# A new order table, and other buffer counts, for a fused gated-recurrence and spatial-gating kernel

## The chip, the cores and the metric

The kernel runs on one core of a Trainium2 chip. The metric is the device time of one execution in microseconds (us); the number given for a kernel is the median of its runs. A core has engines that run side by side, each through its own instruction stream in order: PE (TensorE, matrix products; its weight loads are listed as PEld), DVE (VectorE), ACT (ScalarE), POOL (GpSimd) and SP (SyncE, which here only issues transfers). Engines wait for each other through semaphores. Because a stream is executed in order, an instruction that waits holds back everything behind it on its engine.

## What is computed

The reference has two stages. The first is a gated linear recurrence over 768 steps for 4 batches of 8 heads of width 48; the second is a gated unit whose gate mixes the 768 positions with one 768 x 768 matrix. Cut to what matters:

```python
# stage 1, q, k, v, alpha: [4, 8, 768, 48]
for t in range(768):
    state = alpha[:, :, t, :, None] * state + k[:, :, t] (outer) v[:, :, t]
    y[:, :, t] = q[:, :, t] @ state
x = y.transpose(0, 2, 1, 3).reshape(4, 768, 384)
# stage 2, w_in [384, 1024], w_spatial [768, 768], w_out [512, 384]
h = maximum(x @ w_in, 0)
u, v = h[..., :512], h[..., 512:]
v_n = (v - mean(v)) / sqrt(var(v) + 1e-6)          # over the 512 features
v_s = einsum('ts,bsd->btd', w_spatial, v_n) + b_spatial[None, :, None]
out = (u * v_s) @ w_out
```

## The kernel before

Stage 1 is cut into chunks of 128 steps, six to a batch, 24 in all (numbered 0 to 23). The first eight chunks are loaded and worked on two at a time, as pairs 0 to 3 (function `pair`, line 414); the others singly (function `first`, line 625). For a chunk or a pair the steps are these.

- Four loads: `ac` (alpha), `kc`, `qc`, `vc` (lines 432 and 637, issued by SP). A pair's load is 384 KB, a single chunk's 192 KB. Each name has three buffers that hold two chunks.
- ACT takes the logarithm of alpha (`la`, L443). PE forms its running sums (`cump`, L452). ACT takes two exponentials of them, `binv` (L460) and one in place (L469). `kt` is k times the first (L474, POOL or DVE), `qt` is q times the second (L481, DVE).
- PE transposes `kt` and `qt` (L502), and DVE or ACT copies the results out as `kqT` (L198, L200). PE forms the scores (`sc`, L574), which DVE masks into `ptm` (`m`, L585). PE adds the chunk's contribution to the state (`updq`, L536 and L544). DVE adds the state before to it (`z`, L328, L330), POOL scales it (`S`, L335) and copies it for PE as `sbd` (`sb`, L200).
- PE forms the chunk's output from `ptm` and from the state (`ya`, L601, and `y`, L614). It is copied out (`xs`), transposed (`xt`, L365), and copied into `xT` (`xe`), which is x transposed, ready for stage 2.

For single chunks the same steps stand at L651 to L773, with DVE's `ptm` at L756, `kt` at L681 and `qt` at L691.

Stage 2 works per batch, all its products through one helper line (L819). `v` (24 products in three parts, `second_v`, line 858) makes a tile `v_sb` of 128 positions by 512 features. Its statistics are taken on DVE (`bn`, L884, L885; on ACT for four of them) and ACT (`rs`, L908), and DVE makes the normalised `vn` (L916) of it. `u` (32 products, `second_u`, line 933) makes `uT`. `s` (32 products, each in two halves of three parts, `second_s`, line 945) multiplies `vn` with the transposed spatial matrix `w_spT`. DVE adds the bias into `vsb` (L967), and POOL or DVE multiplies by `uT` into `gT` (`g`, L980). `o` (24 products, `second_o`, line 1017) multiplies with `w_out`. Its result is copied out and stored (L1037; the last tile in two halves, L1011). A matrix part with 512 columns moves 512/384 of the columns of the others.

Weights arrive in fp32 through two buffers called `raw_w` (`NRAW`, line 159) in six loads of 768 KB: `w_in` half 1 (for `v`), `w_in` half 0 (for `u`), `w_sp` 0, 1, 2 (two row blocks each of the spatial matrix), `w_out` (L1084). Each is cast to bf16 in pieces on POOL, ACT or DVE. A load into a buffer waits until the casts of the load before it in the same buffer are done. The spatial rows are transposed by PE (`wt`, L831) and copied out (`we`). `raw_w` buffers are later used for output tiles.

Nothing is scheduled when the kernel is built. Every step is an operation with a number, and the table `PLAN` (line 57) lists all 1156 in the order in which they are emitted: a letter for the engine (P, D, A, G for POOL, S for SP, Q for the landing of a transfer) and the number. The order on each engine is the order of its letters in the table. Numbers behind a colon add filler products to a PE operation: an fp32 product of a constant tile `junk`, of so many columns, that writes into the bank which the operation takes next (L188). Nothing reads its result; it is in PE's stream ahead of the operation. A filler shows as two matmuls in the trace.

Of the kernel before, what the change touches and what calls it, by code (L numbers as in the profile page):

```python
# [57 lines left out]
D0 S49 Q50 D7 D13 S109 Q110 G47 Q48 D11 S51 Q52 G9 D3 S55 Q56 D1 G8 D15 D17 G14 D6 D4 D2 D12 G16 S53 Q54 A57 S113 Q114  # L58
G18 A117 P118:512:512:192 S111 Q112 P68 A119 P262 A69 P58 S19 Q20 P264 G71 A59 P128 A120 A60 G61 S115 Q116 A70 D62
A129 D72 A265 D5 S178 Q179 A263 D122 A130 P126:512:512:512 D132 S180 Q181 G131 P76 P74 P64 P66 D75 G63 A65 D77 G73 D67  # L60
D127 G121 P89:504 P134 S182 Q183 D90 P136 P78 A135 D91 A137 P86 S184 Q185 G133 D80 A23 P124 D88 P149 A79 A125 G81 D87
A123 S322 Q323 G22 D83 A186 P92:512 D151 G82 P146 D93 G21 P96 P187 D150 A97 G84 P197 S24 Q25 A188 P94 D148 P138 G85
A95 D147 A189 G190 P98 S326 Q327 P100 A198 D191 A99 G200 A199 D140 P103 S324 Q325 A101 D201 G202 P195 A139 A192 D102
P203 G141 P193 A104 P205 P207 G142 D143 A194 D196 A206 P152 G144 D204 S29 Q30 D105 A330 S382 Q383 G145 P153 P157 P215
A154 D158 G10 P212 A208 A106 D209 P155 P341 D213 A156 G210 P159 P331 D214 A160 P161 A332 D216 G28 P172 A342 D217 G211
A333 A343 D335 G27 P218 A173 D345 G26 A162 P223 P219 D174 P349 A224 P339 S33 Q34 G334 P170 A220 S328 Q329 D350 P225
D163 P221 S384 Q385 P166 G344 A226 A222 P164 D167 A175 P337 P230 D171 A165 A338 D107 P227 D177 A231 D108 S386 Q387
P168 A390 D176 D340 A228 D32 P347 A169 P238 D31 A348 D229 P247 A239 P244 P362 S37 Q38 A245 P236 D248 A246 D249 G35
P240 D364 A237 S424 Q425 P242 A346 D363 G336 A241 P250 G36 D232 P391 A252 P351 A393 A243 D251 S426 Q427 P253 A233 D353
P270 A392 D234 P266 S428 Q429 A352 A255 D235 G354 P274 D254 A395 P275 D356 G355 D396 P271 G394 D276 P267 D272 S388  # L70
Q389 P359 D268 P398 P278 A39 G40 D360 S41 Q42 P279 D361 A399 G277 P256 A400 P259 D280 P365 G273 A432 D258 P405 S430
Q431 D257 A260 D261 P369 P433 A366 G357 P294 D370 S461 Q462 A434 G281 D406 P367 A435 P371 P295 S495 Q496 A372 D407
G397 P290 A437 G358 D296 P376 A368 D438 G269 P401 P408 P291 G436 A409 S499 Q500 P282 A377 D292 P410 A43 S465 Q466 P440
D402 D44 P283 A46 G403 D442 A412 P373 D441 A411 G45 D284 G439 P447 D378 S463 Q464 A469 P418 G297 A374 P470 D449 S467
Q468 P306 A503 G293 A471 D419 P504 P298 S497 Q498 A472 A307 D448 G285 A505 P420 D375 S592 Q593 A474 G404 P286 A507
D475 P443 A299 S598 Q599 G473 P287 D508 A421 P413 D444 S626 Q627 D288 G445 P416 A414 S501 Q502 G506 P450 A417 P422
D415 A451 S596 Q597 G476 P477 A379 P510 G289 P452 A423 D478 P302 S594 Q595 D453 A512 D479 G446 P480 D511 A600 S705
Q706 P484 D481 A454 P513 A303 D485 P601 G482 P314 A602 D486 G483 A634 P310 D514 S663 Q664 G509 A603 A315 P487 D515
G607 A605 P455 S667 Q668 A488 D606 A311 P516 D381 S665 Q666 A456 P489 D380 P318 A517 D604 S630 Q631 A490 D457 P518
A491 P608 A520 P611 S707 Q708 A519 P492 D319 A671 A458 D609 P521 S628 Q629 D610 A493 D459 P615 A522 D460 P528 D612  # L80
A494 D617 P672 G613 P532 A523 S709 Q710 D529 P635 A673 D616 P544 S777 Q778 A674 A713 G675 P530 D524 A676 P534 S632
Q633 A637 A636 D677 G614 P540 A525 S669 Q670 P714 A533 D526 P548 A639 D527 P560 S711 Q712 A531 D638 A716 P541 A715
D640 S873 Q874 P545 A718 G717 D542 A535 P549 S749 Q750 D546 P618 P561 D719 G547 A619 S743 Q744 D550 P642 A785 P679
D562 A641 P620 G543 P552 S779 Q780 A643 D644 P645 D622 P553 A621 G720 D680 S747 Q748 A681 D646 G678 P649 D554 P721
G647 S877 Q878 P686 D650 A722 P623 G551 D651 S781 Q782 P682 P556 A624 D683 P557 A723 D687 G684 P652 G555 D558 P536
S879 Q880 A653 D688 P537 A751 G648 S745 Q746 P654 P728 D538 G563 A656 P786 P724 D655 S783 Q784 P689 D730 A787 P564
G539 A690 D729 S907 Q908 P752 D725 P691 G685 A754 A789 P576 S946 Q947 A692 D790 A753 P565 D788 S875 Q876 P657 A756
G755 D693 A577 D566 P731 S944 Q945 A758 D757 P568 G559 A732 D625 S1023 Q1024 A658 P792 P759 G726 A569 P733 D794 P694
# [16 lines left out]
A1086 P1097 A1094 D1088 P1101 D1087 P1109 D1092 P1110 P1121 D1111 P1106 G1112 P1102 D1107 P1114 D1103 P1117 D1108  # L105
G1104 P1118 D1115 P1098 D1119 P1122 G1116 D1099 P1125 D1123 P869 D1100 G1124 P1126 D870 P1136 G1120 D1127 S871 Q872
P1128 D1137 P1148 A1129 S1138 Q1139 P1140 D1149 S1130 Q1131 P1132 A1141 S1150 Q1151 P1144 S1142 Q1143 A1133 P1152
S1134 Q1135 A1145 A1153 S1146 Q1147 S1154 Q1155
"""


# [1048 lines left out]
```

## Time and profile before

| | |
|---|---|
| median of 3 runs | 141.3 us (141.24 to 141.33) |
| span of the profiled execution | 144.3 us |
| PE busy | 136.8 us (95%) |
| DVE busy | 118.7 us (82%) |
| ACT busy | 106.8 us (74%) |
| POOL busy | 86.8 us (60%) |
| moved by DMA | 28.64 MB, mean 198 GB/s |

The profiled execution is 3.0 us longer than the median of the runs shown; its span is from its first instruction to its last, the stretch before the first load and the end of the program included. A timeline line gives start, duration, engine, source line, operation, tiles written and read, the number of instructions merged into it, and in brackets the idle time ahead of it with what ended it. A line of the windows view gives, for a stretch, the length, the busy time of PE, PEld, DVE, ACT and POOL with instruction counts, PE's granted clock, the DMA engines' mean busy share, and GB/s. A matmul's recorded duration runs on after the next one has begun, so a matmul's pace is read from starts, or from the length of a run of many.

### The profile page before, as it was taken

The numbers are of one execution on the slowest core, as the hardware profiler recorded it, in microseconds if no ns is written. First come the engines' busy times: TensorE is split into PE (matmuls) and PEld (weight loads), VectorE is DVE, ScalarE is ACT, GpSimd is POOL, SyncE is SP. The second block draws the span as 40 slices with busy tenths as digits, with TensorE's granted clock in tenths as the row PEclk, the third lists the DMA queues.
The fourth block names the chain that finished last, engine by engine and source line by source line (L and its number), as shares of the span: only waits on it lengthen the run. The fifth ranks groups of instructions, "written<-read, shape, count | busy, mean of one in ns | idle before, by whom it ended". The sixth has DMA issues, their size and how long they took to land.

```text
span 144.3 us, 4963 instructions
## 1 busy us (share of the span) xinstructions
PE 136.8 (95%) x1915; PEld 84.2 (58%) x1915; DVE 118.7 (82%) x289; ACT 106.8 (74%) x278; POOL 86.8 (60%) x152
## 2 busy tenths in 40 slices
PE   7799999799799999999999999999999999999990
PEld 3334766656465765676556665665657666555560
DVE  7015798899999969899999999999979897987940
ACT  3473479899895879899997789998797698861031
POOL 6856179892709979981249789511599687002820
PEclk9999999999999999999999999999999999999998
DMA  4999999929899989999899899799999241090055
GB/s 108 321 326 351 282 250 325 344 58 259 181 269 191 300 164 182 205 181 214 169 211 222 175 174 185 152 204 196 212 239 227 66 172 55 0 354 28 5 191 191
DMA packets 89000, 28.64 MB, mean 198 GB/s; under 512 B 83728, under 2 KB 87440, under 8 KB 88976
## 3 DMA queue, kind: packets, MB, share of 16 engines
q1 hardware_dynamic: 88944, 28.32, 79.5%
q8 instruction: 15, 0.25, 0.7%
q14 instruction: 9, 0.07, 0.1%
q0 software_dynamic: 32, 0.00, 0.0%
HBM read 23.60 MB, written 4.72 MB: 196 GB/s over the span
## 4 chain that ended last, share of the span: by engine, by line
PE 78%; DVE 8%; ACT 5%; DMA 3%; issue 3%; SPq 0%; ACTq 0%; DVEq 0%
PE bank L819 47%; PE bank L188 4%; DMA ac<-in_alpha_dram 3%; PE bank L710 3%; PE bank L452 2%; PE bank L502 2%; PE bank L745 2%; PE bank L574 2%; DVE ptm L756 2%; PE bank L773 2%; PE bank L731 2%; PE bank L544 1%; DVE ptm L585 1%; PE bank L657 1%; PE bank L601 1%
## 5 line engine op out<-in xcount | busy, mean ns | idle before, releaser
L819 PE MATMUL bank<-w_spT,vn 128*128 128x384 bf16 x192 | 36.3, 326 | 0.1
L980 POOL TENSOR_TENSOR gT<-vsb,uT 128x384 bf16<-128x384 f32 x28 | 25.7, 927 | 11.7 <-DVE vsb L967 11.2
L335 POOL TENSOR_TENSOR state<-state,bc 128x192 f32<-128x192 f32 x20 | 10.3, 513 | 21.4 <-DVE state L328 6.2
L819 PEld LDWEIGHTS <-vn 128*128 128x128 bf16 x192 | 17.1, 97 | 10.2 <-issue 0.2
L756 DVE TENSOR_TENSOR ptm<-bank,mask 128x512 bf16<-128x512 f32 x32 | 20.8, 682 | 1.0 <-ACT xT L198 1.0
L819 PE MATMUL bank<-xT,w_in 128*128 128x384 bf16 x96 | 19.4, 326 | 0.0
L967 DVE TENSOR_TENSOR vsb<-bank,bsp_bc 128x384 f32<-128x384 f32 x31 | 16.7, 554 | 3.2 <-PE bank L819 2.8
L819 PE MATMUL bank<-w_in,xT 128*128 128x512 bf16 x72 | 18.8, 379 | 0.0
L198 ACT COPY kqT<-bank 128x512 bf16<-128x512 bf16 x24 | 13.6, 590 | 6.9 <-PE bank L502 4.4
L819 PE MATMUL bank<-w_out_sb,gT 128*128 128x384 bf16 (+1 forms) x100 | 18.4, 320 | 0.1
L681 POOL TENSOR_TENSOR kt<-kc,binv 128x384 bf16<-128x384 f32 x13 | 12.0, 927 | 6.6 <-ACT bc L676 2.7
L200 POOL CAST sbd<-state 64x192 bf16<-64x192 f32 x40 | 13.6, 341 | 2.1
L884 DVE BATCH_NORM_STATS2 stats<-v_sb 128x6 f32<-128x512 bf16 x20 | 13.6, 681 | 0.5 <-ACT v_sb L204 0.5
L204 ACT ACTIVATE v_sb<-bank 128x512 bf16<-128x512 f32 x20 | 11.9, 608 | 1.6 <-PE bank L819 1.6
L198 ACT CAST x_sb<-bank 128x384 bf16<-128x384 f32 x21 | 10.2, 493 | 3.5 <-PE bank L773 2.7
L819 PEld LDWEIGHTS <-w_in 128*128 128x128 bf16 x96 | 8.7, 97 | 6.0
L188 PE MATMUL bank<-junk 128*128 128x512 f32 (+2 forms) x16 | 11.1, 838 | 1.1 <-DVE halves_of L264 1.1
L200 DVE COPY kqT<-bank 128x512 bf16<-128x512 bf16 x24 | 9.2, 415 | 3.1 <-PE bank L502 2.3
L819 PEld LDWEIGHTS <-gT 128*128 128x128 bf16 x100 | 8.7, 97 | 5.1 <-POOL gT L980 0.2
L204 ACT ACTIVATE uT<-bank 128x384 bf16<-128x384 f32 x23 | 11.3, 495 | 0.3 <-PE bank L819 0.2
L198 ACT COPY xT<-bank 128x192 bf16<-128x192 bf16 (+1 forms) x27 | 9.1, 378 | 2.4 <-PE bank L365 1.5
L585 DVE TENSOR_TENSOR ptm<-bank,mask 128x512 bf16<-128x512 f32 x16 | 10.2, 682 | 0.7 <-PE bank L574 0.4
(128 smaller groups left out, 285.2 us busy)
## 6 DMA issues: line engine op xcount, KB each, us to landing
ac<-in_alpha_dram SPq DMA_DIRECT2D x16, 192.0 KB, 3.9
kc<-in_k_dram SPq DMA_DIRECT2D x16, 192.0 KB, 4.2
qc<-in_q_dram SPq DMA_DIRECT2D x16, 192.0 KB, 4.0
vc<-in_v_dram SPq DMA_DIRECT2D x16, 192.0 KB, 3.8
raw_w<-in_moe_w_spatial_dram SPq DMA_DIRECT2D x3, 768.0 KB, 4.5
out_dram<-raw_w SPq DMA_DIRECT2D x11, 192.0 KB, 2.0
out_dram<-o_sb SPq DMA_DIRECT2D x9, 192.0 KB, 1.9
ac<-in_alpha_dram SPq DMA_DIRECT2D x4, 384.0 KB, 5.5
```

What stands on the lines that cost most here:

```text
L188: nc.tensor.matmul(out=flat[:, 0:cols].rearrange("p (a b) -> p a b", a=4), lhsT=junk, rhs=junk[:, None, 0:n].to_broadcast([128, 4, n]), st ...
L198: nc.scalar.copy(out=out, in_=in_)
L200: ENG[eng].tensor_copy(out=out, in_=in_)
L204: nc.scalar.activation(out=out, in_=in_, func=AF.Relu)
L335: ENG[eng].tensor_tensor(out=st["state"], in0=st["state"], in1=st["bc"][:, :, None].to_broadcast([128, HP, D]), op=ALU.mult)
L585: nc.vector.tensor_tensor(out=st[f"ptm{par}"][:, s], in0=st[f"pt{s}{par}"], in1=mask2[:, par], op=ALU.mult)
L681: ENG[eng].tensor_mul(out=k_blocks(kt3)[:, :, :, 0:D], in0=quad(st["kc"]), in1=st["binv"])
L756: nc.vector.tensor_tensor(out=st["ptm"][:, s], in0=st[f"pt{s}"], in1=mask4, op=ALU.mult)
L819: return lambda ps: nc.tensor.matmul(out=out(ps), lhsT=lhsT(), rhs=rhs(), start=start, stop=stop)
L884: nc.vector.bn_stats(out=stats, in_=d["v_sb"][:, tt, :])
L967: nc.vector.tensor_tensor(out=hold["vs"], in0=ps[:, 0:TH], in1=bsp_bc[:, th, :], op=ALU.add)
L980: ENG[eng].tensor_tensor(out=bt[b]["gT"][:, dsl, cols], in0=hold["vs"], in1=bt[b]["uT"][:, dsl, cols], op=ALU.mult)
```

## The change

- `NRAW` goes from 2 to 3: three buffers for arriving weights. A weight load then waits for the casts of the third load before it.
- `xT` and `uT` get two buffers each in place of three. The copies into `xT` then wait for the products of `v` and `u` two batches back (`x_users`), and the copies into `uT` for `g` two batches back.
- `v_sb` is no longer one tile for a batch with two buffers, but a tile for each pair of position blocks, with five buffers (`v_tile`). A copy into it waits for the `vn` of five pairs back (`v_users`).
- `PLAN` is another table. The operations and their numbers are the same, 300 of them on PE. Their order on each engine, the engine of those that can run on several, and the fillers differ.

```diff
-    NRAW, NROW, KEEP = 2, 3, 11
+    NVS = 5
+    NRAW, NROW, KEEP = 3, 3, 11
+    def x_users(b):
+        return got(*[("v", b - 2, t, "mm", 0) for t in range(NT)],
+                   *[("u", b - 2, ft, th, "mm", 0) for ft in range(NDS) for th in range(2)])
-                got(("xt", i)) + [made.get(("all", b - 3))], prio=P + 9, use=[sls[r]]))
+                got(("xt", i)) + x_users(b), prio=P + 9, use=[sls[r]]))
-        d["xT"] = batch.tile([128, NCH, KS, C], BF16, name="xT")
-        d["uT"] = batch.tile([128, NDS, S], BF16, name="uT")
-        d["v_sb"] = batch.tile([128, NT, DH], BF16, name="v_sb", bufs=2)
+        d["xT"] = batch.tile([128, NCH, KS, C], BF16, name="xT", bufs=2)
+    def v_tile(b, tt):
+        k = ("v_sb", tt // 2)
+        if k not in bt[b]:
+            bt[b][k] = batch.tile([128, 2, DH], BF16, name="v_sb", bufs=NVS)
+        return bt[b][k][:, tt % 2]
+    def v_users(b, tt):
+        n = b * NT // 2 + tt // 2 - NVS
+        return got(*[("vn", 2 * n // NT, 2 * n % NT + x) for x in range(2)]) if n >= 0 else []
+            if "uT" not in bt[b]:
+                bt[b]["uT"] = batch.tile([128, NDS, S], BF16, name="uT", bufs=2)
```

The table, written with the names of the operations (pair or batch, then block). The order of the first loads on SP, before and after:

```
before  ac.0 ac.1 kc.0 vc.0 qc.0 qc.1 kc.1 w_in.1 vc.1 ac.2 kc.2 qc.2 vc.2 ac.3 w_in.0 qc.3 kc.3
        w_sp.0 ac(chunk 8) w_sp.1 vc.3 kc(8) qc(8) w_sp.2 ...
after   ac.1 ac.0 vc.0 kc.0 qc.1 qc.0 kc.1 ac.2 vc.1 qc.2 kc.2 vc.2 w_in.1 ac.3 w_in.0 qc.3 kc.3
        w_sp.0 w_sp.1 vc.3 ac(8) w_sp.2 qc(8) kc(8) vc(8) ...
```

The first operations on PE, with the columns of fillers in brackets ahead of the operation that they precede (k and q: transposes; the last figure is the even or odd half of a pair):

```
before  [512 512 192] cump.1.0 cump.0.1 bias cump.0.0 bias cump.1.1 [512 512 512] q.1.0 q.0.1 k.0.1 k.0.0 q.0.0
        [504] sc.0.1 k.1.1 q.1.1 updq.0 sc.0.0 k.1.0 sc.1.1 [512] ya.0 sc.1.0 y.1 cump.2 xt.0 updq.1 xt.1
        v.0.0 v.0.1 q.2.0 k.2 q.2.1 updq.2 ya.1 y.2 y.3 sc.2.1 sc.2.0 xt.2 cump.3 xt.3 v.0.2 v.0.3 ya.2 ...
after   [512 192 128] cump.1.0 [128] cump.0.1 [128] cump.0.0 [256 192] bias cump.1.1 [192] k.0.0 updq.0
        [192] q.1.0 k.0.1 q.0.0 [128] q.0.1 bias k.1.1 [256] q.1.1 sc.0.0 [128] sc.0.1 k.1.0 cump.2 [64 in it]
        sc.1.1 updq.1 ya.0 y.1 [192] xt.0 [128] xt.1 k.2.0 q.2.0 q.2.1 sc.1.0 k.2.1 [64] updq.2 sc.2.0
        [128] sc.2.1 ya.1 y.2 v.0.1 y.3 xt.2 v.0.0 cump.3 ya.2 ...
```

In both, 26 to 28 PE operations behind ya.2, with all of batch 0's `u` and `v` products done, come the first `s` products of batch 0. On DVE the order from the first `qt` on is, after the change: three `qt`, z.0, one `qt`, two `kqT`, z.1, the four `ptm` of pair 0, one `kqT`, `qt`, `ptm`, z.2, `qt`, `ptm`, z.3, `kqT`, two `ptm`, a cast of `w_in`, two `ptm`, z.4, the last two `ptm` of pair 2, two `xs`, and then the statistics (`bn`) and `vn` of batch 0 with the fourth pair's work between them. Before, the statistics of v.0.0 and v.0.1 stood ahead of pair 2's `ptm`. On POOL the three casts of `w_in.0` come directly behind `sb.4` after the change; before, one was ahead of it.

At the end, PE's last operations were o.3.3, o.3.1, o.3.4 and the second half of o.3.5; after the change o.3.3, both halves of o.3.5, o.3.4. Over the whole table these operations change engines: 13 `kqT` copies of stage 1 from DVE to ACT and 7 back, five `g` from POOL to DVE and one back, six `o` copies from DVE to ACT and three back, eight `u` copies from DVE to ACT and five back, five `xs` from ACT to DVE and two back, and a few others; `g` on DVE goes from 3 to 7.

More of the change, by code (lines that the diff above doesn't have):

```diff
@@ L63 @@
[L63 to L77, printed above, removed]
@@ L916, in vn @@
                     nc.vector.tensor_scalar(
-                        out=d["vn"][:, t, :], in0=d["v_sb"][:, t, :],
+                        out=d["vn"][:, t, :], in0=v_tile(b, t),
                         scalar1=d["mvs"][:, t, 0:1], scalar2=d["rstd"][:, t:t + 1],
@@ L925, in vn @@
                 nc.gpsimd.tensor_scalar(
-                    out=d["vn"][:, t, :], in0=d["v_sb"][:, t, :], scalar1=d["rstd"][:, t:t + 1], scalar2=nb,
+                    out=d["vn"][:, t, :], in0=v_tile(b, t), scalar1=d["rstd"][:, t:t + 1], scalar2=nb,
                     op0=ALU.mult, op1=ALU.add)
```

102 lines of the change are left out of this document (59 added, 43 removed).

## The prediction

> **What bounds the kernel now.** I read the page's chain first, then stretches of 14 us, then the chain's pieces in order of time, then single engines in the first 45 us. From the windows view, with the chain's last long piece:
>
> ```profile
> span 144.3 us, 4963 instructions
> PE 78%; DVE 8%; ACT 5%; DMA 3%; issue 3%; SPq 0%; ACTq 0%; DVEq 0%
> 0.00:14.00 14.00, 12.05 (x22) 4.82 (x23) 5.23 (x25) 7.12 (x13) 9.26 (x24) 1.00 0.96 275
> 14.00:28.00 14.00, 13.36 (x329) 9.46 (x328) 11.79 (x26) 10.47 (x25) 9.49 (x20) 1.00 1.02 297
> 28.00:42.00 14.00, 12.64 (x199) 7.92 (x200) 13.30 (x30) 12.19 (x33) 7.83 (x12) 1.00 0.71 192
> 56.00:70.00 14.00, 14.00 (x210) 8.81 (x208) 13.20 (x33) 12.77 (x39) 8.74 (x16) 1.00 1.01 196
> 84.00:98.00 14.00, 13.87 (x214) 8.60 (x211) 13.32 (x35) 13.39 (x41) 8.30 (x15) 1.00 0.89 180
> 126.00:140.00 14.00, 14.00 (x89) 8.53 (x88) 11.01 (x25) 4.13 (x10) 4.90 (x5) 1.00 0.35 132
> 123.54 17.18 PE bank L819 x105
> ```
>
> There are three stages. At the end PE is dense: 105 matmuls in 17.18 us are 0.164 us each for 384 columns. From about 42 to 123 us PE and DVE are both full (DVE 13.2 to 13.3 of 14 us), and in places ACT too (13.39). Before 42 us PE counts as busy for 38.05 of 42 us, which misleads: part of that is filler. The chain and the engines there:
>
> ```profile
> 35.37 1.84 DVE vn L916 x4
> 37.54 1.25 DVE w_row L200 x2
> 9.97 4.46 PE L188 MATMUL bank<-junk 128*128 128x512 f32 x6
> 14.27 0.61 PE L502 MATMUL bank<-ident,qt 128*128 128x128 bf16 x8
> 31.14 0.81 PE L601 MATMUL bank<-vbp,ptm 64*128 64x48 bf16 x32
> 42.55 2.61 PE L819 MATMUL bank<-w_spT,vn 128*128 128x384 bf16 x15
> 10.31 1.02 DVE L481 TENSOR_TENSOR qt<-qc,bank 128x384 bf16<-128x384 f32 x2 [6.54 <-ACT bank L469]
> 11.73 1.06 DVE L481 TENSOR_TENSOR qt<-qc,bank 128x384 bf16<-128x384 f32 x2
> 15.14 1.42 DVE L200 COPY kqT<-bank 128x512 bf16<-128x512 bf16 x4 [2.35 <-PE bank L502]
> 42.48 0.36 DVE L328 COPY state<-bank 128x192 f32<-128x192 f32 x1
> ```
>
> The third `qt` product, which the first transposes need, is through about 0.5 us after 11.73, at 12.2. PE reaches them at 14.27, since the filler of 1536 columns ahead of them lasts until then. DVE idles 2.35 us for it. After that DVE is the engine with least slack up to the first `s` product at 42.55; `vn` and a cast of a spatial row on DVE are on the chain there. So there are two things to forecast: when this first stage ends, and whether the full middle keeps what it gains.
>
> **The change part by part.** First, the start. Loads and clock:
>
> ```profile
> 1.23 4.23 DMA ac<-in_alpha_dram
> 4.24 0.84 ACT L443 ACTIVATE la<-ac 128x768 bf16<-128x768 f32 x1 [2.21 <-DMA ac<-in_alpha_dram]
> 9.42 1.25 ACT L469 ACTIVATE bank<-bank 128x384 f32<-128x384 f32 x3
> 8.48 0.91 POOL L474 TENSOR_TENSOR kt<-kc,binvp 128x384 bf16<-128x384 f32 x1 [1.58 <-ACT binvp L460]
> 6.97 0.84 PE L452 MATMUL bank<-la,le_pair 128*128 128x384 bf16 x2
> 21.41 0.49 PE L452 MATMUL bank<-la,le_pair 128*128 128x384 bf16 x2
> 15.38 1.06 PE L188 MATMUL bank<-junk 128*128 128x504 f32 x2
> ```
>
> The table before begins with `cump.1.0`, whose load is the second to arrive; after the change that load is the first, so the sum needs only the first `la`, done at 5.08, and can begin at about 5.3 behind 832 columns of filler (an estimate from the 1536 columns above). ACT then has seven exponentials and casts of 0.42 us (1.25 for three) ahead of the first `qt`, from about 7.1: the first `qt` starts near 10.1, as before. The gain is behind it. PE now has only `k.0.0`, `updq.0` and 192 columns ahead of the first `qt` transposes, and `kt` is there by about 9.6, so they come at 11 to 11.5 in place of 14.27, and DVE's 2.35 us go.
>
> The fillers behind the first sum are not fewer: 2496 columns in place of 2552, in sixteen pieces. At 1.06 us for 504 columns they take 5.2 us, at the 4.46 us for 1536 they take 7.2. I cost them at nothing, because DVE's work below covers them. Without that cover PE would need, from 5.3 to `ya.2`, its own 13.4 us (the order table's eight sums at 0.32, twelve transposes, six scores, three updates and the rest at their paces before) and about 5 of filler, so up to 24: PE trails DVE by only 1.5 us there.
>
> Two 384-column sums are 0.32 us apart at 6.97 (0.84 less one matmul's 0.52) and 0.16 at 21.41: PE runs at half pace early, though the granted clock in the window reads 1.00. Long filler before `qt` ended the slow phase; the small ones might do it later. A bound: at half pace PE soon has no gaps, so a delay of one more stretch like the 4.46 us one at half pace costs at most some 2 us, partly under DVE; and below nothing, as PE is fed from about 2.4 us on with hardly a gap until 11, some 2 us gained. I take 0, halfway. On this the Trainium skill, "TensorE: Matmul & The Clock Gate", Part 1 on the clock gate, says that the clock doubles after about 3.4 us of sustained activity in a free-running window; the 4.46 us filler just ahead of the first fast products agrees. By it the full clock would come by about 9 us here if the small fillers leave no gap, and the sum below would gain up to 1 us more; if the gaps break each window, it is the clock rival below.
>
> Second, DVE up to `z.6`, the last step at 42.48. Its groups between 10 and 43 us:
>
> ```profile
> L585 DVE TENSOR_TENSOR ptm<-bank,mask 128x512 bf16<-128x512 f32 x14 | 8.9, 682 | 0.7 <-PE bank L574 0.4 <-issue 0.3
> L481 DVE TENSOR_TENSOR qt<-qc,bank 128x384 bf16<-128x384 f32 x8 | 4.2, 545 | 7.1 <-ACT bank L469 7.1
> L200 DVE COPY kqT<-bank 128x512 bf16<-128x512 bf16 x8 | 3.0, 413 | 2.3 <-PE bank L502 2.3
> L330 DVE TENSOR_TENSOR state<-bank,state 128x192 f32<-128x192 f32 x4 | 1.4, 349 | 0.1
> L206 DVE TENSOR_SCALAR uT<-bank 128x384 bf16<-128x384 f32 x2 | 1.0, 552 | 0.1
> L200 DVE COPY w_spT<-bank 128x384 bf16<-128x384 bf16 x3 | 0.9, 332 | 0.0
> 42.84 0.74 DVE L916 TENSOR_SCALAR vn<-v_sb,mvs,rstd 128x512 bf16<-128x512 bf16 x2
> ```
>
> Before, from the first `qt` to the end of `z.6`: 42.84 - 10.31 = 32.5 us. After, the same stretch of DVE's order has one `kqT` less (0.38), no `uT` copies (1.0), one `w_spT` less (0.3), and the memsets that stood between the two rows of `qt` (from 11.33 to 11.73, 0.4) come earlier, but there are two `vn` more (0.74) and a cast of v (0.33, as the nearest copy): 1.0 us less. With the 2.35 us of idle time gone that is 29.15. The new order packs `ptm` groups that depend on POOL and ACT; new waits can be 0 (all inputs early) to 2.5 (as much as the idle time removed); I take 0.8, nearer to 0 because the other idle times in these rows sum to little over 1. So `z.6` ends at 10.1 + 29.95 = 40.05, a gain of 2.8.
>
> PE against this: to the end of pair 2's `ptm` DVE has 6 `qt` (3.15), 12 `ptm` (7.6), 4 `kqT` (1.5), 5 `z` (1.75) and a cast (0.6), 14.6 us, so 24.7 and with waits 25.5 to 27.2, where `ya.2` came at 31.14. From there PE has 10.5 us to the first `s`: 8 `u` at three times 0.164, 4 `v` at 0.655, the rest small; with 320 columns of filler and 0.5 to 1.5 us of waits it ends at 37.2 to 39.9, against 42.55, with 14.9 - 13.4 = 1.5 us more work left at `ya.2` already in it. That is 2.7 to 5.3 us gained; I keep DVE's 2.8, since DVE is full in the next stage too.
>
> Third, weights and SP.
>
> ```profile
> SPq L1084 <- POOL w_in L200: 6.0, 1, 6.0
> 29.78 0.73 POOL L200 CAST sbd<-state 64x192 bf16<-64x192 f32 x2
> 30.57 1.17 POOL L200 CAST w_in<-raw_w 128x512 bf16<-128x512 f32 x2
> ```
>
> SP stood 6.0 us at `w_sp.1` for a cast of `w_in` with `vc.3` and the next chunks' loads queued behind it. With three buffers that wait is for `w_in.1`, and goes. It takes at most POOL's wait for the row cast off the path, and part of the first stage's gain contains it: 0 on top. `w_in.1` now comes behind five more pair loads. Twelve of them and itself are 5.5 MB; at 275 GB/s for 14 us and 297 after, it lands near 19.6, and `w_in.0` (6.7 MB) near 23.6; the first `v` product is placed where PE arrives at about 23. Costed 0; its bad end is the slower rival.
>
> Fourth, the other buffers. `v_sb` of pair n waits for `vn` of pair n-5, two batches' worth of order behind it less one pair; `xT` and `uT` wait for work of two batches back. In the table each lies tens of operations before its need: 0, by the middle stage's length.
>
> Fifth, the middle. Net moves by the rows above: DVE loses six `kqT` (2.25), three `u` (1.5), three `o` (1.5), two `kt` and three `w_spT` (1.9), and gains four `g` (2.2), three `xs` (1.6), four casts of v (1.3): some 2 us less, of which 1.0 is counted. ACT gains some 4 us, where one window has 0.6 free and another 1.2. From -1.0 (all DVE relief arrives) to +2.5 (ACT's share of it waits in order); I take 0.
>
> Sixth, the end.
>
> ```profile
> out_dram<-o_sb SPq DMA_DIRECT2D x9, 192.0 KB, 1.9
> out_dram<-raw_w SPq DMA_DIRECT2D x2, 96.0 KB, 1.7
> 139.45 0.48 ACT L198 COPY raw_w<-bank 128x384 f32<-128x384 f32 x1 [0.50 <-PE bank L819]
> 138.80 0.36 DVE L200 COPY raw_w<-bank 128x192 f32<-128x192 f32 x1 [0.42 <-PE bank L819]
> ```
>
> The last store is a whole tile: 1.9 for 1.7, its copy 0.48 for 0.36, but it no longer queues behind one: +0.2 (-0.3 to +1.0, if DVE with four `g` more at the end holds an `o`).
>
> Sum: -2.8 + 0.2 = -2.6 us, 144.3 to 141.7 in the profile's terms; the profiled execution stands 3.0 above the median shown, which I keep: 141.3 - 2.6 = **138.7**.
>
> **The rivals.** (a) *Given back in the middle.* For it: PE, DVE and ACT full together, and 4 us more on ACT. Against: DVE's work shrinks. With +1.8 of the 2.5: 140.5. (b) *More.* No new waits at the start (-0.8), the clock early (-1), DVE's relief (-0.6): 136.3. (c) *Slower: `w_in.0` on POOL.* Its three casts stand behind `sb.4`, and PE's `u.0.1.0` waits in order for them, with four `v` and seven `u` behind it. DVE's `z.4` comes in my walk at 24.2 to 25.9; `S`, `sb` and casts of 0.6 each make that 27.3 to 29. Between that `u` and the first `s` lie 9.8 us of work and filler and 1 of waits, so it decides from 31.7 on. If `sb.4` is as late as before (29.78 + 0.73), the casts end at 32.35, `s` starts at 43.15, and the time is 141.3 + 0.6 + 0.2 = 142.1. Against it: DVE has less ahead of `z.4`. (d) *The change doesn't do what it says*: the pairs ahead of `w_in` finish early but the middle's order sets the end anyway, all is hidden: 141.3. For it: stores and `o` products are spread late; against: the middle has no slack to absorb an early start. (e) *The clock late*: +1.6 of the 2 on the sum, 140.3.
>
> **How the numbers follow.** Forecast (own range 137.3 to 140.1) 0.48; (a) 0.17, of which 0.02 no change; (b) 0.09; (c) 0.18; (d) 0.04; (e) 0.04. About 0.2% is what a measurement tells from no change. Faster: 0.48 + 0.15 + 0.09 + 0.04 = 0.76; same 0.06; slower 0.18. The range 136.0 to 142.2 leaves out a third of (b) and half of (c).
>
> **What would show it.** Right: DVE's wait for the first transposes under 1 us; the last `ptm` of pair 2 before 28; the first `s` product at 38.5 to 40; SP without the 6 us wait; windows after that as full as now. Wrong: `w_in` casts on POOL past 31.7, half-pace sums after 14 us, or the first `s` early and the end not.

## The result and the profile after

After the change the kernel takes 144.44 us (median of 4 runs, 144.12 to 144.71) where the kernel before, on the same chip, takes 141.28 (4 runs, 141.24 to 141.33). The ratio is 1.0219 with an interval of 1.0201 to 1.0237: slower by 3.2 us, where 138.7 was forecast. The profiled execution after is one of these runs, 144.57 us with a span of 142.8. A run's time is its span and 1.7 to 1.8 us here and in every run below.

The page after, its span and the chain's shares by engine:

```profile
span 142.8 us, 4998 instructions
PE 60%; ACT 14%; DVE 13%; issue 5%; DMA 3%; SPq 2%; POOL 1%; POOLq 0%; DVEq 0%; ACTq 0%
```

The windows view of after, in three of the stretches of 14 us shown for before (length, then PE, PEld, DVE, ACT, POOL, PE's clock, DMA share, GB/s):

```profile
0.00:14.00 14.00, 11.59 (x116) 8.49 (x116) 7.64 (x30) 9.15 (x18) 9.16 (x24) 1.00 0.99 270
...
56.00:70.00 14.00, 13.93 (x189) 8.51 (x188) 11.87 (x32) 13.73 (x42) 6.98 (x12) 1.00 0.95 187
...
84.00:98.00 14.00, 13.58 (x188) 7.95 (x186) 12.95 (x30) 12.64 (x38) 8.55 (x15) 1.00 0.96 194
```

PE's share of the chain fell from 78% to 60%, and ACT's rose from 5% to 14%. In 56 to 70 us ACT is busy for 13.73 of 14 us (12.77 before). In 84 to 98 us PE is short by 0.42 us where it was short by 0.13.

The timeline after, PE's first sums, the first `qt` transposes, `ya.2`, the first `s` product and the last group of matmuls:

```profile
6.35 0.85 PE L458 MATMUL bank<-la,le_pair 128*128 128x384 bf16 x2
...
7.36 0.33 PE L458 MATMUL bank<-la,le_pair 128*128 128x384 bf16 x1
7.52 0.33 PE L458 MATMUL bank<-la,lt_pair 128*128 128x384 bf16 x1
...
11.13 0.39 PE L508 MATMUL bank<-ident,qt 128*128 128x128 bf16 x4
...
26.50 0.57 PE L607 MATMUL bank<-vbp,ptm 64*128 64x48 bf16 x32
...
39.23 1.15 PE L823 MATMUL bank<-w_spT,vn 128*128 128x384 bf16 x6
...
138.68 0.65 PE L823 MATMUL bank<-w_out_sb,gT 128*128 128x384 bf16 x3
```

The start went as forecast: the transposes come at 11.13 in place of 14.27, and the first `s` at 39.23 in place of 42.55. Two sums are 0.32 us apart at 6.35 (0.85 less 0.53) and 0.16 at 7.36, so PE goes from half pace to full pace near 7 us; below, this is called the opening of its clock. In the execution of before that was profiled it was still at half pace at 9.97, where 1536 columns of filler took 4.46 us.

So by the traces shown, after is the faster: 142.8 against 144.3. The runs say the opposite. The execution of before that was profiled was none of the runs at 141.3: with the 1.8 us its time would be 146.1. Executions of before differ, in the main by when the clock opens (e0, e4 and e5 below), so that beside the later experiments its runs lie anywhere from 141.25 to 147.23 us, and ratios are formed with the undisturbed ones among them. After itself was run only where before stayed at 141.24 to 141.33; how far its runs spread elsewhere is not known.

### The profile page after: what moved, and what is told of

It is laid out like the page before. It is cut to its first block, busy times and chain, and to the rows that moved or that the text cites. A ratio compares the mean times of both kernels' runs of the same rounds, so it can differ in the third digit from the quotient of the medians.

```text
span 142.8 us, 4998 instructions
## 1 busy us (share of the span) xinstructions
PE 134.7 (94%) x1939; PEld 87.0 (61%) x1939; DVE 119.3 (84%) x286; ACT 111.0 (78%) x286; POOL 82.8 (58%) x147
## 4 chain that ended last, share of the span: by engine, by line
PE 60%; ACT 14%; DVE 13%; issue 5%; DMA 3%; SPq 2%; POOL 1%; POOLq 0%; DVEq 0%; ACTq 0%
PE bank L823 38%; DMA kc<-in_k_dram 3%; DVE stats L900 3%; PE bank L716 2%; DVE ptm L762 2%; PE bank L508 2%; PE bank L189 2%; PE bank L751 2%; PE bank L779 2%; DVE vn L932 2%; PE bank L395 2%; PE bank L737 2%; SPq L438 2%; PE bank L773 2%; ACT v_sb L205 1%
## 5 line engine op out<-in xcount | busy, mean ns | idle before, releaser
L999 POOL TENSOR_TENSOR gT<-vsb,uT 128x384 bf16<-128x384 f32 x24 | 21.7, 918 | 17.2 <-DVE vsb L986 17.0
L687 POOL TENSOR_TENSOR kt<-kc,binv 128x384 bf16<-128x384 f32 x15 | 13.8, 930 | 13.0 <-PE bank L666 7.5
L199 ACT COPY kqT<-bank 128x512 bf16<-128x512 bf16 x30 | 16.9, 600 | 2.0 <-PE bank L716 1.5
L205 ACT ACTIVATE uT<-bank 128x384 bf16<-128x384 f32 x26 | 12.6, 502 | 1.0 <-PE bank L823 0.8
L189 PE MATMUL bank<-junk 128*128 128x128 f32 (+4 forms) x40 | 11.0, 384 | 2.4 <-DVE junk L1069 2.4
L199 ACT CAST x_sb<-bank 128x384 bf16<-128x384 f32 x18 | 8.6, 488 | 4.3 <-PE bank L779 2.2
L189 PEld LDWEIGHTS bank<-junk 128*128 128x128 f32 x40 | 7.8, 225 | 4.3 <-DVE junk L1069 2.4
```

The lines of the kernel that those rows point to most:

```text
L189: nc.tensor.matmul(out=flat[:, 0:cols].rearrange("p (a b) -> p a b", a=4), lhsT=junk, rhs=junk[:, None, 0:n].to_broadcast([128, 4, n]), st ...
L199: nc.scalar.copy(out=out, in_=in_)
L205: nc.scalar.activation(out=out, in_=in_, func=AF.Relu)
L687: ENG[eng].tensor_mul(out=k_blocks(kt3)[:, :, :, 0:D], in0=quad(st["kc"]), in1=st["binv"])
L999: ENG[eng].tensor_tensor(out=bt[b]["gT"][:, dsl, cols], in0=hold["vs"], in1=bt[b]["uT"][:, dsl, cols], op=ALU.mult)
```

## The experiments

All readings of the traces in one table, in us. "First s" and "last" are the starts of the first `s` product and of the last matmul of the profiled execution, and "between" is their difference. It holds the same products in all kernels but for twelve transposes of a spatial row (0.2 to 0.3 us), which the new order has behind the first `s`.

| kernel | runs: median (range, count) | span | first s | last | between |
|---|---|---|---|---|---|
| before, the profile shown | | 144.3 | 42.55 | 140.79 | 98.24 |
| after | 144.44 (144.12 to 144.71, 4) | 142.8 | 39.23 | 139.01 | 99.78 |
| e0 before again | 142.64 (1) | 140.9 | 39.01 | 137.32 | 98.31 |
| e1 new buffers, old order | 144.67 (141.34 to 145.55, 10) | 139.9 | 38.11 | 136.40 | 98.29 |
| e2 new start, old rest | 144.02 (143.61 to 144.17, 4) | 142.4 | 40.60 | 138.84 | 98.24 |
| e3 old start, new rest | 147.23 (146.75 to 147.51, 4) | 145.4 | 37.80 | 141.58 | 103.78 |
| e4 old, long first filler | 141.44 (141.21 to 141.88, 10) | 139.7 | 37.88 | 136.11 | 98.23 |
| e5 old, no first filler | 144.40 (144.06, 144.74) | 143.0 | 41.18 | 139.41 | 98.23 |
| e6 new, few fillers | 143.31 (142.95 to 144.83, 4) | 141.1 | 37.78 | 137.35 | 99.57 |
| e7 new, third pair first | 145.33 (145.20 to 145.50, 4) | 143.7 | 40.30 | 139.87 | 99.57 |
| e8 old, fewer fillers | 144.30 (142.43 to 148.07, 6) | 140.7 | 37.61 | 137.12 | 99.51 |
| e9 new order, old engines | 149.78 (149.40 to 150.48, 4) | 147.6 | 39.44 | 143.79 | 104.35 |
| e10 new until batch 2 | 145.62 (145.18 to 146.58, 4) | 144.0 | 39.62 | 140.42 | 100.80 |
| e11 new, gapless start | 143.47 (142.80 to 146.86, 8) | 143.8 | 40.47 | 140.05 | 99.58 |
| e12 one cast on ACT | 143.85 (142.94 to 146.42, 12) | 142.5 | 39.59 | 138.73 | 99.14 |
| e13 three casts off DVE | 144.21 (143.61 to 144.54, 7) | 142.3 | 39.12 | 138.50 | 99.38 |

### The reference: e0, e4 and e5

e0 is the kernel before, unchanged. e4 and e5 change one entry of its table, the filler ahead of the first sum:

```diff
-P118:512:512:192      (before: 1216 columns ahead of cump.1.0)
+P118:512:512:512      (e4)
+P118                  (e5)
```

> The kernel before, unchanged, for one more profile. The changed kernel's runs are 1.8 us longer than their spans (144.57 and 142.8), while the profile of before that the prediction used spans 144.3 us, 3.0 more than its runs. Theory A (that profile shows an unusual execution, in which PE stayed at half pace until 13.4 us): this one spans 139 to 140 us, the sums (L452) are 0.16 us apart by about 9 us, and the first spatial product starts at 37.5 to 38.5. Theory B (profiles of this kernel are simply 3 us longer than its runs): again about 144.3, and the first spatial product near 42.5.

> The kernel before with one number changed: the filler ahead of the first sums has 512+512+512 columns in place of 512+512+192, so that PE has no gap from 1.06 us to the first sums at 6.4. Theory A (a run of before takes 141.3 or up to 146 us by when PE's clock opens, which needs a stretch without a gap): the clock opens by 8 us in every run, and all runs take 141.2 to 142.3. Theory B (the spread has another cause): runs spread from 141.3 to 146 as those of before do beside it.

> The kernel before without the filler ahead of the first sums, so that PE has no work before 6.4 us. Theory A: the clock opens late in every run, between 9.5 and 14 us; 144 to 146.5 us, the first spatial product at 41 to 43. Theory B: as before beside it, 141.3 in some runs.

The timeline of e0 (PE's sums, its filler ahead of the first `qt` transposes, these, and the first `s`):

```profile
6.62 0.49 PE L452 MATMUL bank<-la,le_pair 128*128 128x384 bf16 x2
...
8.34 2.74 PE L188 MATMUL bank<-junk 128*128 128x512 f32 x6
11.38 0.62 PE L502 MATMUL bank<-ident,qt 128*128 128x128 bf16 x8 [0.30 <-DVE qt L481]
...
39.01 2.77 PE L819 MATMUL bank<-w_spT,vn 128*128 128x384 bf16 x16
```

And DVE's in e0, its wait for the first transposes and a later one for a load:

```profile
12.26 1.41 DVE L200 COPY kqT<-bank 128x512 bf16<-128x512 bf16 x4 [0.40 <-PE bank L502]
...
20.96 0.56 DVE L481 TENSOR_TENSOR qt<-qc,bank 128x384 bf16<-128x384 f32 x1 [0.57 <-DMA qc<-in_q_dram]
```

The same code, another execution: PE is at full pace at 6.62, so the same filler takes 2.74 us in place of 4.46, and PE then waits for `qt` on DVE rather than DVE for PE. The 2.35 us that DVE stood idle in the first profile are 0.40 here, and the first `s` comes 3.5 us earlier. From there on all the traces of before's table with its middle unchanged are alike (before, e0, e1, e4, e5): 98.2 to 98.3 us to the last matmul. Theory A's bands are missed, though, by 0.9 us in the span and 0.5 in the first `s`.

The timelines of e4 and e5, the filler and the sums, and the first `s` product:

```profile
1.06 5.49 PE L188 MATMUL bank<-junk 128*128 128x512 f32 x6 [1.06 <-DVE halves_of L264]
...
6.73 0.49 PE L452 MATMUL bank<-la,le_pair 128*128 128x384 bf16 x2
...
37.88 3.10 PE L819 MATMUL bank<-w_spT,vn 128*128 128x384 bf16 x18
```

```profile
9.24 0.82 PE L452 MATMUL bank<-la,le_pair 128*128 128x384 bf16 x2
9.85 4.84 PE L188 MATMUL bank<-junk 128*128 128x512 f32 x6
...
41.18 0.50 PE L819 MATMUL bank<-w_spT,vn 128*128 128x384 bf16 x2
```

With 320 columns more, PE is fed without a gap from 1.06 us to its first sums, the clock is open in time, and all ten runs lie between 141.21 and 141.88, while before beside it spread from 141.29 to 145.28. Without the filler the sums at 9.24 are still 0.3 us apart (0.82 for two), the next filler takes 4.84 us, and the two runs take 144.06 and 144.74. Both results are in theory A's bands. A filler of 1536 columns takes 5.49 us at half pace (e4's first) and 2.74 at full pace (e0), so by an estimate from these the clock opened near 13.4 us in the execution of before that was profiled (4.46 us) and near 14.0 in e5 (4.84).

So most of the difference between 141.3 and 146 is the clock at the start, and 141.3 is before with an early clock. Not all of it: in e0 the clock is open as early as in e4, and its first `s` is still 1.13 us later. The first transposes are 0.18 us behind e4's (11.38 and 11.20), and the rest comes in waits between there and 26 us, the longest 0.57 us for a load (20.96); what made these longer than in e4 is not known.

The Trainium skill, "TensorE: Matmul & The Clock Gate", Part 1, says that the clock opens after about 3.4 us of sustained activity in a window that runs freely, and so differs from run to run. The traces agree that it differs; but in e5 PE was at work from 6.26 us with hardly a gap, and by the estimate above the clock opened 7.8 us later. The Trainium skill puts the cost of it below 1% of a typical span; between the two traces of before it is 3.5 of 142 us, 2.5%, and the measurement decides.

### Buffers or order: e1, e2 and e3

e1 keeps the changed code (`NRAW`, `xT`, `uT`, `v_sb`) and puts the old table in:

```diff
 (after's code)
-PLAN = after's table
+PLAN = before's table
```

e2 has after's table up to the first `s` product, then the remaining operations in before's order and on before's engines; e3 is the reverse.

> The changed kernel's code and buffers with the order table of before. Theory A (the order is the cause): 141.3 us, within 0.3. Theory C (two buffers for xT and uT, or the five v tiles, add waits): slower, up to the whole 3.1 us, 144.4.

> The new table up to the first spatial product of batch 0 (its first 290 entries), then all other operations in the order of before. Theory A1 (the new start is slower than a usual start of before by 1 to 2 us, the rest of the loss lies behind it): 142.3 to 143.3. If the whole loss is in the start: 144.4. If none is (loss all in the middle and the end): 141.3 or less.

> The order of before up to the first spatial product (295 entries), then all other operations in the order of the new table. Theory A1: 142.3 to 143.3 (the middle and end of the new table cost 1 to 2 us). Loss all in the start: 141.3. Loss all behind it: 144.4 or more.

Three of e1's runs take 141.34 to 141.74 us, the others 144.53 to 145.55, as before's beside it do (141.35 to 146.01); the ratio is 0.9966 (0.9898 to 1.0033), and its trace has the old 98.29 us between. The buffers cost nothing and bring nothing with the old order, so what is lost comes with the table. What they are worth to the new order is not shown: no run has the new table with the old buffers.

e2 shows 98.24 between: behind the first `s`, the old order is as short as ever. Its first `s` is 1.4 us later than after's, probably because operations of two orders meet there (which of them was not looked for), so its 144.02 us, in none of the bands, says little about the start. e3's middle, 103.78, can't be read at all: at the join PE stood 1.40 us for a spatial row at 40.78, and the clock fell back for one stretch (nine `s` matmuls took 3.04 us from 42.10, 0.34 each). Runs at 146.75 to 147.51.

### The fillers: e6 and e7

e6 is after without the fillers behind `k.0.0` in its table. These are 1600 columns of 3328; the expectations for e6 and e11 count 1536.

```diff
-P126:192 ... P76:128 ... P136:256 ... P89:128
+P126 ... P76 ... P136 ... P89
... (and eight more entries)
```

e7 keeps the fillers and moves the third pair's output (`ya.2`, `y.5`, `y.4`) on PE ahead of `v.0.0` and `cump.3`, since DVE stands idle for it in after:

```profile
23.63 1.27 DVE L591 TENSOR_TENSOR ptm<-bank,mask 128x512 bf16<-128x512 f32 x2
25.14 0.56 DVE L201 CAST x_sb<-bank 128x384 bf16<-128x384 f32 x1 [0.23 <-PE bank L620]
27.38 0.56 DVE L201 CAST x_sb<-bank 128x384 bf16<-128x384 f32 x1 [1.69 <-PE bank L620]
```

> The changed kernel without the fillers behind the first transposes (1536 of its 3328 columns are left out, the five pieces up to the running sums and the first transposes stay). Theory D (the fillers between 10 and 29 us stand on PE's path, 3.0 us of the chain there): 142.0 to 143.4, the first spatial product at 37.5 to 38.5. Theory E (they only fill waits): 144.4 within 0.3, as the prediction had it; slower if PE falls back to half pace.

> The changed kernel with PE's output products of pair 2 (ya.2, y.5, y.4) ahead of the second v product and the fourth pair's sums, whose inputs came later. Theory F (DVE's 1.7 us of idle time at 25.7 to 27.4, waiting for them, is what the new start loses): 143.0 to 143.9, the first spatial product about 1 us earlier. Theory E (that wait is covered by other waits): 144.4 within 0.3.

The timeline of e6, the same cast on DVE, and the first `s` on PE:

```profile
26.18 0.56 DVE L201 CAST x_sb<-bank 128x384 bf16<-128x384 f32 x1 [1.17 <-PE bank L620]
```

```profile
37.78 1.14 PE L823 MATMUL bank<-w_spT,vn 128*128 128x384 bf16 x6
```

Without 1600 columns of filler the third pair's output comes 1.20 us earlier (26.18 for 27.38), and the first `s` 1.45 us earlier. So these fillers stood on the path, as theory D has it: PE was late, and DVE waited for PE. Without them the new start is as early as the old one with an early clock (37.78, and 37.88 in e4), and no earlier. Whether they have a use is open. e6's runs spread over 1.9 us, the slowest at a mean granted clock of 0.972, where e7, which keeps the fillers, stays within 0.3 on the same chip; but e12 keeps them too and spreads over 3.5.

e7 shows a wait moved, not removed. DVE in e7:

```profile
26.08 0.56 DVE L201 CAST x_sb<-bank 128x384 bf16<-128x384 f32 x1 [0.39 <-PE bank L620]
27.52 0.69 DVE L900 BATCH_NORM_STATS2 stats<-v_sb 128x6 f32<-128x512 bf16 x1 [0.89 <-ACT v_sb L205]
...
29.56 1.02 DVE L487 TENSOR_TENSOR qt<-qc,bank 128x384 bf16<-128x384 f32 x2 [1.13 <-ACT bank L475]
```

The 1.69 us became 0.39, and then DVE stood 0.89 for the statistics of `v.0.0` and 1.13 for the fourth pair, both of which now come later from PE. The first `s` comes at 40.30, 1.07 us later than in after, and the runs at 145.33 miss both bands: 0.9 slower than after. What DVE lacks there is not one product ahead of another but PE's time.

### The middle: e9 and e10

e9 is after with 80 operations behind the first `s` put back on the engine that they had before, each at its place in the new order. e10 is after up to the first `s` of batch 2, and before's table from there.

> After, with every operation behind the first s product put back on the engine that it had before (80 operations: copies of kqT and its pieces, xe, u, o, g, kt, v casts), each at its place in the new order. Start unchanged: first s at 39 to 39.5. Theory G (the 1.3 to 1.5 us that the new order loses between the first s and the last product come from ACT's 4 us of added work and from work put on other engines): first s to last product back to 98.2 to 98.7, runs at 142.9 to 143.6. Theory H (they come from where operations stand in the order, mostly PE's own): 99.3 to 100.8, as the new places were made for the new engines, runs at 144.0 to 145.5.

> After's order and engines up to the first s product of batch 2 (101 us), before's from there on. First s at 39 to 39.5. Theory H1 (the loss of the middle is made in batches 0 and 1, from the first s to 101 us): first s to last product 99.2 to 99.8, end stretch shorter by 0.25, runs at 143.8 to 144.4. Theory H2 (it is made evenly, or mostly in batches 2 and 3): 98.2 to 98.8, runs at 142.8 to 143.4.

e9 misses both bands: 104.35 us between, 149.78. The old engines in the new order cost 4.6 us, so moving all operations back repairs nothing; whether some of the new engines cost is not shown by it. e10 misses both too, with 100.80 between. Behind its join PE stands once for long, where neither after nor e1 has a wait over 0.3 us in the whole middle:

```profile
106.08 1.14 PE L823 MATMUL bank<-w_spT,vn 128*128 128x384 bf16 x6 [1.11 <-DVE qt L697]
```

Without this wait it would be 99.7, in H1's band and far from H2's. An estimate from PE's products, each counted at the median pace of its shape, is less sharp: after lags behind e1 by 0.7 to 0.8 us from 30 to 50 us behind the first `s`, by 0.8 to 1.2 from 55 to 75 (batch 2's `s` begins at about 62), and by 1.3 to 1.5 from 80 on. So more of the loss is made ahead of batch 2 than behind it, but not clearly all. The windows view of after and of e1, each from its first `s` to its last matmul:

```profile
39.23:139.01 99.78, 98.95 (x1349) 61.51 (x1346) 89.21 (x207) 78.32 (x212) 57.87 (x95) 1.00 0.74 167
```

```profile
38.11:136.40 98.29, 98.03 (x1338) 61.50 (x1332) 87.96 (x208) 75.95 (x208) 60.05 (x97) 1.00 0.77 174
```

PE's marked idle time is 0.83 us in after and 0.26 in e1, so 0.57 of the 1.5 us stands there as waits; the rest is in products that start later without a wait that the trace marks.

### Casts of v under POOL: e12 and e13

The change puts four casts of v more on DVE, and one of the fourth pair. After's timeline, three of them beside what POOL did:

```profile
36.81 0.98 POOL L201 CAST w_row<-raw_w 128x768 bf16<-128x768 f32 x1 [1.92 <-DMA raw_w<-in_moe_w_spatial_dram]
37.02 0.98 DVE L201 CAST vbp<-vc 128x384 bf16<-128x384 f32 x1
...
85.24 2.77 POOL L999 TENSOR_TENSOR gT<-vsb,uT 128x384 bf16<-128x384 f32 x3
86.16 1.08 DVE L201 CAST vb<-vc 128x384 bf16<-128x384 f32 x1
87.30 0.36 PE L737 MATMUL bank<-vb,kt 128*128 128x48 bf16 x8 [0.26 <-DVE vb L201]
...
89.90 0.35 DVE L201 CAST vb<-vc 128x384 bf16<-128x384 f32 x1
...
101.27 1.90 POOL L687 TENSOR_TENSOR kt<-kc,binv 128x384 bf16<-128x384 f32 x2 [3.58 <-issue]
101.66 0.74 DVE L201 CAST vb<-vc 128x384 bf16<-128x384 f32 x1
```

The same cast takes 0.35 us at 89.90 and 0.74 to 1.08 in three other places. At 37.02 it ends at 38.00, 0.21 us behind POOL's cast, which began first and ends at 37.79. At 86.16 it began just behind the second of POOL's three products (86.12 to 87.03 in the trace) and ended 0.2 us behind that one. At 101.66 it ended at 102.40, 0.2 us behind the first of POOL's two (102.19). So the cast stood until POOL's instruction was through. The Trainium skill, "SBUF — State Buffer", section "SBUF: two separate sides", says that DVE, in some of its fast modes, and POOL exclude each other on a shared pair of ports for the length of a whole instruction; the three ends agree. One cast does not show it: at 61.42 it took 0.35, though POOL began one at 61.41.

e12 moves chunk 16's cast, the longest, to ACT; e13 chunk 19's too, and the fourth pair's (chunk 6) to POOL:

```diff
-D758   (cast of v, chunk 16, on DVE)
+A758   (on ACT)
-D922   D336   (chunk 19, chunk 6: e13 only)
+A922   G336
```

> After with one letter changed: the cast of v of chunk 16 on ACT (as before the change) in place of DVE, at its place in the order. In after it took 1.09 us on DVE at 86.16 where others take 0.35, under a product of POOL's that ran from 86.12 to 87.03, and PE then stood 0.26 us for it. Theory P (DVE's cast stood while POOL's instruction ran, and this is part of the 1.3 to 1.5 us that the middle lost): DVE's 1.09 us go, PE's lag at the third batch falls by 0.3 to 0.7 us, first s to last product 99.1 to 99.5 (after 99.78), runs at 143.6 to 144.1. Rival M (ACT is as full there, the wait only moves to it): 99.6 to 100.2, runs at 144.2 to 144.8.

> As the one before, and two more casts of v taken off DVE: chunk 19's to ACT (0.74 us at 101.66 in after, under POOL's product from 101.27 to 102.19) and chunk 6's to POOL (0.98 us at 37.02, under POOL's cast from 36.81 to 37.79). 0.74 + 0.39 + 0.63 = 1.76 us above 0.35 each go from DVE. Theory P: first s product up to 0.4 us earlier than 39.23, first s to last product 98.6 to 99.4, runs at 142.9 to 143.8. Rival M: 99.5 to 100.2, runs at 144.0 to 145.

The timeline of e12 around the cast, and of the next one on DVE:

```profile
85.59 2.66 POOL L999 TENSOR_TENSOR gT<-vsb,uT 128x384 bf16<-128x384 f32 x3
...
86.76 0.54 ACT L199 CAST vb<-vc 128x384 bf16<-128x384 f32 x1
87.35 0.36 PE L737 MATMUL bank<-vb,kt 128*128 128x48 bf16 x8
...
89.12 0.92 POOL L687 TENSOR_TENSOR kt<-kc,binv 128x384 bf16<-128x384 f32 x1
89.48 0.77 DVE L201 CAST vb<-vc 128x384 bf16<-128x384 f32 x1
```

Theory P's band holds in the trace: 99.14 us between for 99.78, and PE no longer waits, though the next cast now falls under a product of POOL's itself (0.77, ending 0.21 behind POOL's 90.04). How much the one letter is worth is less sure: e6, e7 and e11, which have after's order behind the first `s` and the cast on DVE, show 99.57 to 99.58, so it is 0.4 to 0.6 us by one trace. e13 gives 99.38, at the upper edge of P's band and not better than e12: the gains don't add, and its first `s` is 0.11 us earlier where up to 0.4 was expected. By the runs neither is a clear gain over after: e12's median is 143.85, in P's band, but its twelve runs spread over 3.5 us on a chip where before spread too; e13's is 144.21, in M's band.

### Versions meant to be better: e8 and e11

e8 is before with e4's first filler and 1528 columns fewer behind it. e11 is after with the memset of `junk` first on DVE, 1536 columns ahead of `cump.1.0`, and e6's fillers out.

```diff
 (e8, before's table)
-P118:512:512:192 ... P126:512:512:512 ... P89:504 ... P92:512
+P118:512:512:512 ... P126:512:512 ... P89 ... P92
```

```diff
 (e11, after's table)
-S109 Q110 D5 ... D4 G14 D0 ... P118:512:192:128 ...
+D0 S109 Q110 D5 ... D4 G14 ... P118:512:512:512 ...
```

> Before with four numbers of its order table changed: the filler ahead of cump.1.0 in three pieces of 512 (as in e4), the one ahead of the first qt transposes 1024 columns instead of 1536, and none at sc.0.1 (504) and ya.0 (512): 1528 columns less behind the first sum, some 3.2 us of PE at 1.06 us for 504. A version meant to beat both kernels. Theory D (fillers behind the first sum stand on PE's path, as e6 showed for the new order with -1.45 us for 1536 columns): first s product at 36.5 to 37.5 where e4 had it at 37.88, and runs at 140.0 to 141.0. Theory A (what matters is only when PE's clock opens, and DVE sets the rest of the start): first s within 0.3 us of 37.88 and runs at 141.1 to 141.7. If the clock opens later or falls back without the cover, runs spread from 141 to 146.

> After with its start repaired by what e4 and e6 showed: the memset of the filler's tile first on DVE, 1536 columns of filler ahead of cump.1.0 in place of 832, and none behind tr.k.0.0 (1536 columns out, as in e6). If the start's price is fillers and clock, the clock opens by 7 us in every run and the first s product comes at 37.3 to 38.5 (after 39.23, e6 37.78 with the clock at 8.41), and the runs lie within 1 us of each other. Theory H (the order behind the first s costs 1.3 to 1.5 us, whatever the start): first s to last product 99.3 to 99.9, runs at 142.3 to 143.8, still behind before's 141.3. Rival (the middle's loss comes from the late start, and a good start repairs it): 98.2 to 98.6, runs at 141.0 to 142.2.

e8's runs miss both bands. Its first `s` comes 0.27 us earlier than e4's (37.61), just within theory A's 0.3, and then 1.3 us are lost in the middle, about half of them at one place. DVE there in e8, and in e1:

```profile
81.69 0.55 DVE L691 TENSOR_TENSOR qt<-qc,bank 128x384 bf16<-128x384 f32 x1 [1.02 <-DMA qc<-in_q_dram]
```

```profile
81.01 0.55 DVE L697 TENSOR_TENSOR qt<-qc,bank 128x384 bf16<-128x384 f32 x1 [0.30 <-ACT bank L692]
```

A `qc` had not landed in e8; in e1 DVE waited for ACT, 0.7 us less. The load took 3.80 us, as in e4, but was issued at 77.79 us, in e4 at 76.64; why SP came to it later, though the first `s` was earlier, is not settled. Its other runs go up to 148.07. Four of the six have a mean granted clock of 0.985 to 0.988, of before's eleven runs beside it two (0.988), so the clock seems to fall back more often without these fillers. e11's trace shows one such fall. Its PE, around 24 us, and its windows view:

```profile
22.14 0.55 PE L607 MATMUL bank<-vbp,ptm 64*128 64x48 bf16 x30
24.15 0.22 PE L607 MATMUL bank<-vbp,ptm 64*128 64x48 bf16 x2 [1.46 <-issue]
...
24.61 1.48 PE L823 MATMUL bank<-w_in,xT 128*128 128x512 bf16 x3
...
27.59 0.33 PE L458 MATMUL bank<-la,le_pair 128*128 128x384 bf16 x1
27.75 0.33 PE L458 MATMUL bank<-la,lt_pair 128*128 128x384 bf16 x1
```

```profile
24.00:27.40 3.40, 3.04 (x18) 1.83 (x19) 1.38 (x3) 1.82 (x3) 2.63 (x6) 0.51 0.95 281
```

PE stood idle for 1.46 us, and the clock went back to half: three `v` matmuls took 1.48 us where after's take 0.81, until the sums at 27.59 are 0.16 apart again. What PE waited for is not in the trace ("issue"). At the same place it stood 0.47 us in after, and 0.18 in e6, which lacks the same fillers, so the wait itself is not put down to them. In this execution the first `s` came at 40.47. Five of e11's eight runs take 142.80 to 143.77 at a mean granted clock of 0.995 to 1.0, the other three 145.61 to 146.86 at 0.965 to 0.987. So they don't lie within 1 us of each other; the five lie in theory H's band, and none of the eight in the rival's. With 99.57 between in e6, whose first `s` is at 37.78, and 99.58 in e11 at 40.47, the middle's loss does not depend on the start. No version here beats before at its best; e4 keeps before there.

## Why the prediction was wrong

**The execution that the sum was made against: the step that failed most.** The prediction read: "the profiled execution stands 3.0 above the median shown, which I keep". That takes the 3.0 us as a constant of the profile. They were the thing itself: an execution with a late clock, 4.8 us of time above the median (146.1 for 141.3), whose lateness lay in the main just where the change saves. The prediction had the signs in hand, the two sums 0.32 us apart at 6.97 and the filler's 4.46 us, and used them for a rival only. With the clock open by 7 us DVE's idle time is 0.40 (e0) and not 2.35, and the first `s` stands at 37.9 to 39.0 (e0, e1, e4). Against the profile shown, after's first `s` is 3.3 us earlier; against e4's, which is before at 141.4, it is 1.35 later.

**The start, against its own profile: right, with one term wrong.** The forecast was a gain of 2.8, with `s` at 38.5 to 40; it came at 39.23. The first `qt` started where it was put:

```profile
9.96 1.48 DVE L487 TENSOR_TENSOR qt<-qc,bank 128x384 bf16<-128x384 f32 x3 [0.50 <-ACT bank L475]
```

The transposes came at 11.13 (11 to 11.5 forecast), `ya.2` at 26.50 (25.5 to 27.2). The failed step is "I cost them at nothing, because DVE's work below covers them", of the fillers. e6 measured 1.45 us for 1600 of the 2496 columns. The reserve of 1.5 us that the prediction gave for this was PE's lead over DVE at `ya.2` by estimate; in fact PE was behind there, and DVE waited 1.69 us for it (27.38).

**Weights, SP and buffers: right.** SP's longest wait in the first 45 us is now 2.2 us, in place of 6.0:

```profile
SPq L438 <- POOL vbp L201: 2.2, 1, 2.2
```

e1 confirms that the buffers cost nothing with the old order. The slower rival (c) did not occur: POOL cast `w_in.0` directly behind `sb.4`, and the casts ended at 27.59, far from 31.7. Its load came 2.3 us later than the 23.6 reckoned, as POOL still waited 0.70 us for it:

```profile
25.86 1.73 POOL L201 CAST w_in<-raw_w 128x512 bf16<-128x512 f32 x3 [0.70 <-DMA raw_w<-in_moe_w_in_dram]
```

**The middle: 0 taken, 1.5 measured.** That is inside the bounds given (-1.0 to +2.5) and near rival (a)'s 1.8. Two parts of it are known. A spatial row's transposes moved behind the first `s`: 0.2 to 0.3. And "four casts of v (1.3)", priced by the nearest copy at 0.33 each, was mis-sized: one took 1.08, and moving it gained 0.4 to 0.6 on PE's path (e12). With the casts the account of DVE fails too: "some 2 us less" was forecast, and DVE's busy time on the page is 119.3 us in after and 117.8 in e1, 1.5 more, where the three casts held by POOL (e13) make 1.76. ACT's "some 4 us" more is right (111.0 for 106.7). The other 0.6 to 0.9 of the middle is not placed; which waits are its causes was not settled. e9 rules out only that undoing all engine moves at once helps.

**The end: right.** 0.2 forecast; from the last matmul's start to the end of the span it is 3.8 us in after (142.8 - 139.01) and 3.5 in e1 (139.9 - 136.40), 0.25 to 0.3 more.

Put together in the profile's terms: 144.3 - 3.3 + 1.5 + 0.3 = 142.8, the span measured. Against an execution of before with an early clock, e4's trace: 39.23 - 37.88 = 1.35 (the start, where 1.45 of filler stand on the path), 99.78 - 98.23 = 1.55 (the middle) and 0.25 (the end), 3.15 us together; the medians of the runs are 144.44 - 141.28 = 3.16 apart.

**The rivals.** None of them is what happened: (a) had the middle right, (c) the sign for another reason, and (e), the clock late, was argued for the changed kernel, where it was the profile of before that had it.

## What to carry to other kernels

When a profiled execution is some per cent longer than the runs, find where the excess lies before taking any saving from it: a saving at that place may not exist in the runs that are counted. Read the pace of two equal matmuls in the first microseconds for that, not the clock column of the windows view, which read 1.00 there in before and after alike; a later fall does show in it (0.51 in e11). Filler products take PE's time: ahead of the first real work, where PE has nothing else, 320 columns more opened the clock early and took before's spread away (e4); among work that other engines wait for, 1600 columns cost 1.45 us (e6). Whether those later fillers keep the clock from falling back was not settled.

## What was not expected of the hardware

The clock's opening differs by more than 6 us between executions of one program: before's sums are at full pace at 6.62 in e0, and in the profile shown the filler at 9.97 ran at half pace until near 13.4 (the estimate above). A gap of 1.46 us on PE ahead of 24.15, after a stretch of small matmuls, was followed by half pace until close to 27.59 us (e11). And one cast on DVE, 0.35 us alone, took 0.74 to 1.08 us when POOL had begun an instruction just before it, in three of four such places of after and again in e12.
